# A feed-forward layer of 1728 features on a 128 x 128 array: the last 64 features as two token halves in column groups and row groups instead of one padded tile

## The chip, the cores and the metric

The kernel runs on one core of one Trainium2 chip. The metric is the device time of one execution in microseconds (us).

Names used below: PE is TensorE, PEld its weight loads, DVE is VectorE, ACT is ScalarE, POOL is GpSimd. The stationary operand of a matmul is the one that a weight load brings in; the other is the moving one. Results land in one of eight PSUM banks (`ps[:, b, :]`), which this program takes again only after DVE or ACT has emptied it. "L608" is line 608 of the kernel file; a line can be that of a helper that records all matmul groups, so the operand names matter more than the line.

## The reference, cut to what matters

```python
# S = 2048 tokens, D = 640, F = 1728 = 13 * 128 + 64
def _A_ref(x, wqkv, wo):            # linear attention with 32 heads of 20 features
    ...
    return o.reshape(B, S, D) @ wo
def _B_ref(x, w1, w2, w3, w4):
    h = _gelu(_layernorm(x) @ w1)
    ...                             # token shifts, @ w2, residual: x1
    h2 = _gelu(_layernorm(x1) @ w3) @ w4      # 640 -> 1728 -> 640
    return x1 + h2
out = g * a + (1 - g) * b           # g: a gate for each token
```

The change concerns the line with `w3` and `w4`. The hidden size 1728 is 13 full tiles of 128 features and one tile of 64.

## The kernel before

All instructions are recorded in Python, ordered by a list scheduler at build time, and then issued in that fixed order. Matmuls go through one helper. The scheduler's items name what they must follow: `(item, 0.3)` means "0.3 us after that item by the scheduler's own estimate", `(item, None)` means "after it in program order, without a delay".

```python
    def mm_group(out_ap, pairs, reads_extra=()):
            ...
            for i, (l, r) in enumerate(pairs):
                ins = e.matmul(out_ap, l, r, start=(i == 0), stop=(i == n - 1))   # L608
```

The hidden layer is padded to FP = 1792 (KF = 14 tiles, zeros in the last 64 columns of w3 and rows of w4). One w3 group is 5 matmuls of 512 tokens (KD = 5). One w4 tile of 128 tokens is 14 matmuls of 512 output columns and 14 of 128.

```python
    def w3_group(c, j):                       # c: chunk of 512 tokens, j: F tile
        cols = slice(512 * c, 512 * (c + 1))
        ...
        b = bank()
        mm_group(ps[:, b, :], [(w3[:, k, 128 * j:128 * (j + 1)], xnT[:, k, cols]) for k in range(KD)])
        activation(h2T[:, sl, j, :], ps[:, b, :], ACTF.Gelu_apprx_tanh)

    def w4_tile(t):                           # t: tile of 128 tokens
        ...
        b1, b2 = bank(), bank()
        mm_group(ps[:, b1, 0:512], [(h2T[:, sl, k, 128 * a:128 * (a + 1)], w4[:, k, 0:512]) for k in range(KF)])
        mm_group(ps[:, b2, 0:128], [(h2T[:, sl, k, 128 * a:128 * (a + 1)], w4[:, k, 512:D]) for k in range(KF)])
        stt(x_tok[:, t, 0:512], ps[:, b1, 0:512], ...)      # DVE empties the banks
        stt(x_tok[:, t, 512:D], ps[:, b2, 0:128], ...)
```

Next to w4 runs the end of the attention branch. For each token tile DVE normalizes the attention features (`qn_tile`), a DMA transposes them into `pqnT`, and PE multiplies them by `M_sb` (`a_tile`). From tile 4 on, `qn_tile(t)` may start only after `w4_tile(t - 4)`:

```python
    def qn_tile(t):
        tt(dve, qprod[:, :], pq_tok[:, t, :], zb[:, :], ALU.mult)
        ...                                   # reduce, add, reciprocal, multiply: all DVE
        sch.dma("sp", pqnT[:, :, 128 * t:128 * (t + 1)], pq_tok[:, t, :], ..., transpose=True)

    for t in range(NT):
        deps = [(("zb",), 1.0), (("q", max(t, 2)), 2.0), (("w2", NT - 1), 0.5)]
        deps.append((("w3", 0, 3 * t), 0.0) if t < 4 else (("w4", t - 4), 0.0))
        IT.add("QN", ("qn", t), 0.0, lambda t=t: qn_tile(t), deps)
```

## Time and profile before

The kernel before took 269.9 us as the median of 3 runs (269.23 to 270.06).

TensorE is busy 98% of the 268.0 us span and is 94% of the chain. Everything else has slack.

The costliest PE groups of the page: line, engine, operation, operands, shapes, count | busy us, mean ns of one | idle time just before them and what ended most of it.

```profile
L608 PE MATMUL ps<-xnT,w_60 128*128 128x512 bf16 x280 | 63.0, 379 | 0.0
L608 PE MATMUL ps<-w_85,h2T 128*128 128x512 bf16 (+1 forms) x448 | 63.0, 299 | 0.0
L608 PE MATMUL ps<-M_sb,pqnT 128*128 128x512 bf16 (+1 forms) x160 | 24.0, 299 | 0.9 <-DMA pqnT<-pq_tok 0.9
```

The first is w3 (4 chunks x 14 tiles x 5), the second w4 (16 tiles x 28), the third the attention tail. The mean of 379 ns is not what a matmul costs. Matmuls overlap, and what counts is the distance from start to start. The time-ordered view of PE shows it (start us, length us, engine, line, operands, count, and in brackets idle time before):

```profile
133.79 2.75 PE L608 MATMUL ps<-xnT,w_60 128*128 128x512 bf16 x12
...
167.25 0.87 PE L608 MATMUL ps<-M_sb,pqnT 128*128 128x512 bf16 x7
169.04 0.82 PE L608 MATMUL ps<-M_sb,pqnT 128*128 128x512 bf16 x3 [0.93 <-DMA pqnT<-pq_tok]
```

Twelve matmuls in 2.75 us are eleven distances and one duration: (2.75 - 0.38) / 11 = 0.215 us each for 512 columns. In the records a matmul of 128 columns has a distance of 56 ns. Both agree with the formula for an isolated warm matmul, N/2.4 + 2.5 ns, which the Trainium skill gives in "TensorE: Matmul & The Clock Gate", section "Back-to-back issue gap".

The waits of PE in the whole run (what it waited for: us in total, times, longest):

```profile
PE ps L828 <- POOL ones_c L662: 1.6, 1, 1.6
PE ps L608 <- DMA pqnT<-pq_tok: 0.9, 1, 0.9
PE ps L851 <- DMA wq<-in_A_wqkv_dram: 0.2, 1, 0.2
```

The first and last belong to the start. In the 250 us after it, PE waits once, for the transposed tile 4 of `pqnT`. The chain of waits shows the way to it (start us, length us, what):

```profile
163.35 0.74 DVE qprod L636
...
165.57 0.82 DVE pq_tok L1021
166.40 0.03 DVE x_tok L642
166.42 2.58 DMA pqnT<-pq_tok
169.00 0.05 issue
169.04 95.37 PE ps L608 x610
```

Tile 4 of `qn` must follow w4 tile 0, and the scheduler has placed it behind the emptying of w4 tile 1 in DVE's order (the step just before `qprod` in this chain, `x_tok` at 163.00, not shown). After `qprod` come four more DVE instructions and a DMA of 2.58 us. The matmuls at 169.04 need the result.

### The profile page before, as it was taken

Reading aid. Unit: us, or ns where it says so; the run is one execution under the profiler, and the core shown is the slowest. Engines: PE = TensorE matmul, PEld = TensorE weight load, DVE = VectorE, ACT = ScalarE, POOL = GpSimd, SP = SyncE. Lnnn points to the kernel's source line nnn. Section 1 sums busy time; section 2 is a strip of 40 time slices with the busy share of each in tenths; the row PEclk is TensorE's granted clock in tenths of the full one; section 3 lists DMA queues with packets and bytes.
Section 4 is the critical chain, followed back from the end, with each engine's and each line's share of the span. In section 5 each row is a group of like instructions: output and inputs, shape, how many; then the busy total and the mean of one; then the engine's idle time right before and its main releaser. Section 6 shows DMA issues by size and latency. Waiting matters only on the chain.

```text
span 268.0 us, 4324 instructions
## 1 busy us (share of the span) xinstructions
PE 262.3 (98%) x1707; PEld 138.9 (52%) x1707; DVE 155.0 (58%) x308; ACT 95.9 (36%) x184; POOL 102.4 (38%) x155
## 2 busy tenths in 40 slices
PE   7999999999999999999999999899999999999995
PEld 3555555555454556554444455455455455555563
DVE  1497877830005667994009957988663574374733
ACT  1396677743453451614555300003311322230000
POOL 5003995766579294965950020310111011012110
PEclk9999999999999999999999999999999999999999
DMA  6765896649568121414468210214201210310421
GB/s 185 255 100 146 193 182 121 191 82 120 103 122 285 72 49 27 96 26 53 91 141 270 51 24 0 51 24 131 42 1 24 81 55 15 27 24 0 102 72 49
DMA packets 50212, 24.69 MB, mean 92 GB/s; under 512 B 41676, under 2 KB 48781, under 8 KB 50192
## 3 DMA queue, kind: packets, MB, share of 16 engines
q1 hardware_dynamic: 49040, 21.15, 34.8%
q0 software_dynamic: 1152, 3.28, 5.3%
q8 instruction: 13, 0.21, 0.4%
q14 instruction: 7, 0.06, 0.1%
HBM read 11.96 MB, written 2.62 MB: 54 GB/s over the span
## 4 chain that ended last, share of the span: by engine, by line
PE 94%; DMA 3%; DVE 2%; SPq 1%; issue 0%
PE ps L608 84%; PE ps L779 8%; DMA wq<-in_A_wqkv_dram 2%; DMA pqnT<-pq_tok 1%; PE ps L851 1%; SPq L284 1%; PE ps L929 1%; DVE x_tok L642 1%; DVE dnr L1016 0%; DVE pq_tok L1021 0%; DVE qprod L636 0%; PE ps L619 0%; DVE dnr L1020 0%; DVE dnr L630 0%
## 5 line engine op out<-in xcount | busy, mean ns | idle before, releaser
L659 ACT ACTIVATE h2T<-ps 128x512 bf16<-128x512 f32 x56 | 33.4, 597 | 88.3 <-PE ps L608 88.3
L608 PE MATMUL ps<-xnT,w_60 128*128 128x512 bf16 x280 | 63.0, 379 | 0.0
L608 PE MATMUL ps<-w_85,h2T 128*128 128x512 bf16 (+1 forms) x448 | 63.0, 299 | 0.0
L630 POOL TENSOR_SCALAR abx<-x_tok,stg 128x640 f32<-128x640 bf16 x16 | 15.3, 959 | 108.8 <-DVE x_tok L642 37.2
L608 PEld LDWEIGHTS ps<-w_85,h2T 128*128 128x128 bf16 x448 | 35.2, 98 | 28.1
L608 PEld LDWEIGHTS ps<-xnT,w_60 128*128 128x128 bf16 x280 | 26.7, 98 | 29.4
L642 DVE SCALAR_TENSOR_TENSOR x_tok<-ps,stg,abx 128x512 bf16<-128x512 f32 (+1 forms) x32 | 17.2, 549 | 34.5 <-PE ps L608 34.2
L636 DVE TENSOR_TENSOR x_tok<-ps,x_tok 128x512 bf16<-128x512 f32 (+1 forms) x32 | 15.5, 485 | 33.8 <-PE ps L608 32.0
L659 ACT ACTIVATE Er<-ps 128x640 bf16<-128x640 f32 x32 | 22.4, 704 | 19.2 <-PE ps L608 9.8
L659 ACT ACTIVATE hsT<-ps 128x512 bf16<-128x512 f32 (+1 forms) x32 | 18.9, 594 | 24.9 <-PE ps L608 24.5
L608 PE MATMUL ps<-M_sb,pqnT 128*128 128x512 bf16 (+1 forms) x160 | 24.0, 299 | 0.9 <-DMA pqnT<-pq_tok 0.9
L779 PE MATMUL ps<-pk_tok,x_tok 128*128 128x512 bf16 (+1 forms) x160 | 24.2, 299 | 0.0
L608 PE MATMUL ps<-wkg,xT 128*128 128x512 bf16 (+1 forms) x160 | 24.0, 299 | 0.0
L608 PE MATMUL ps<-xnT,w_61 128*128 128x512 bf16 x100 | 23.9, 379 | 0.0
L608 PE MATMUL ps<-w_62,hsT 128*128 128x512 bf16 (+1 forms) x160 | 23.9, 299 | 0.0
L608 PE MATMUL ps<-wq,xT 128*128 128x128 bf16 (+1 forms) x140 | 21.1, 299 | 0.0
L642 DVE SCALAR_TENSOR_TENSOR abx<-ps,stg,abx 128x512 f32<-128x512 f32 (+1 forms) x32 | 17.6, 549 | 6.2 <-PE ps L608 2.4
L636 POOL TENSOR_TENSOR zacc<-zacc,pk_tok 128x640 f32<-128x640 f32 x15 | 20.9, 1396 | 0.4
L608 PEld LDWEIGHTS ps<-M_sb,pqnT 128*128 128x128 bf16 x160 | 13.2, 98 | 12.4 <-DMA pqnT<-pq_tok 1.1
L608 PEld LDWEIGHTS ps<-w_62,hsT 128*128 128x128 bf16 x160 | 13.3, 98 | 12.1
L608 PEld LDWEIGHTS ps<-wkg,xT 128*128 128x128 bf16 x160 | 12.9, 97 | 9.4
L779 PEld LDWEIGHTS ps<-pk_tok,x_tok 128*128 128x128 bf16 x160 | 12.6, 98 | 8.8
(67 smaller groups left out, 248.2 us busy)
## 6 DMA issues: line engine op xcount, KB each, us to landing
w_60<-in_B_w_dram SPq DMA_DIRECT2D x1, 2160.0 KB, 8.1
w_85<-in_B_w_dram SPq DMA_DIRECT2D x1, 2080.0 KB, 8.8
x_tok<-in_A_x_dram SPq DMA_DIRECT2D x3, 640.0 KB, 6.3
out_dram<-x_tok SPq DMA_DIRECT2D x3, 640.0 KB, 3.4
wq<-in_A_wqkv_dram SPq DMA_DIRECT2D x5, 160.0 KB, 4.8
wkg<-in_A_wqkv_dram SPq DMA_DIRECT2D x1, 800.0 KB, 7.3
wv<-in_A_wqkv_dram POOLq DMA_DIRECT2D x1, 800.0 KB, 6.5
wo_aug<-in_A_wo_dram POOLq DMA_DIRECT2D x5, 150.0 KB, 5.0
```

Source lines behind the costliest of these rows:

```text
L284: return e.dma_start(out_ap, in_ap)
L608: ins = e.matmul(out_ap, l, r, start=(i == 0), stop=(i == n - 1))
L630: return engf(lambda e: e.tensor_scalar(out_ap, in_ap, s1, s2, op0, op1), rd, [out_ap], cost=cost)
L636: return engf(lambda e: e.tensor_tensor(out_ap, a, b_, op), [a, b_], [out_ap], cost=cost)
L642: return dve(lambda e: e.scalar_tensor_tensor(out_ap, in0, scalar, in1, op0, op1), rd, [out_ap], cost=cost)
L659: return act(lambda e: e.activation(out_ap, in_ap, func, bias=bias, scale=scale), rd, wr, cost=cost)
L779: ins = e.matmul(o, l, r, start=(t0 + q_ == 0), stop=(t0 + q_ == NT - 1))
L851: ins = e.matmul(o, l, r, start=(k == 0), stop=(k == KD - 1))
L929: ins = e.matmul(o, l, r_, start=st_, stop=sp_, skip_group_check=True)
```

## The change

The intent is to stop multiplying by zeros. The last 64 features fill half of the array, so the other half can work on other tokens at the same time:

- **w3**: the 64 columns of w3 are the stationary operand, once in columns 0 to 63 and once in columns 64 to 127 of the array. Two matmuls of 256 tokens each run side by side. Their results land in two partition halves of one bank.
- **w4**: the contraction has 64 rows. The first token half uses rows 0 to 63, the second rows 64 to 127, with the last 64 rows of w4 loaded twice. One block serves two token tiles and starts four PSUM banks; those banks are held until the 13 full tiles have been added.
- A small third part holds the pair of banks of the kv product until they have been masked.

The diff, cut to its core:

```diff
-KF = FP // 128          # 14
+KFF = F // 128          # 13
+    h2h = rb.alloc("h2h", [128, 2, 256], BF16)
-    w4 = rb.alloc("w4", [128, KF, D], BF16)
+    w4 = rb.alloc("w4", [128, KFF + 1, D], BF16)
...
     def kvt_group(h):
         b = pair()
+        bank_hold.update((b, b + 1))        # released in lt_evac
...
+    def w3_half(c):
+        b = bank()
+        for k in range(KD):
+            xv = xnT[:, k, 512 * c:512 * (c + 1)].rearrange("p (n h q) -> p n h q", h=2, q=128)
+            for par in range(2):
+                jobs.append((ps[64 * par:64 * par + 64, b, 0:256], w3[:, k, 128 * KFF:F], xv[:, :, par, :], ...))
+        ...
+                ins = e.matmul(o, l, r, start=st, stop=sp)                          # L1026
+        activation(h2h[:, sl, :], ps[:, b, 0:256], ACTF.Gelu_apprx_tanh)
...
+    def w4_half(t):                          # t even: tiles t and t + 1
+        bs = [bank() for _ in range(4)]      # all four held
+        for i, (n0, n1) in enumerate(((0, 512), (512, D))):
+            for par in range(2):
+                rows = slice(64 * par, 64 * par + 64)
+                jobs.append((ps[:, bs[2 * par + i], 0:n1 - n0], h2h[rows, sl, 128 * pr:128 * (pr + 1)], w4[rows, KFF, n0:n1]))
+        ...
+                ins = e.matmul(o, l, r, start=True, stop=False)                     # L1078
...
     def w4_tile(t):
-        b1, b2 = bank(), bank()
+        b1, b2 = w4_banks.pop(t)             # 13 tiles, start=False                # L1096
...
-        dma_in(w4[0:64, KF - 1, :], B_w4[128 * (KF - 1):F, :], "w4b")
+        dma_in(w4[0:64, KFF, :], B_w4[128 * KFF:F, :], "w4b")
+        dma_in(w4[64:128, KFF, :], B_w4[128 * KFF:F, :], "w4c")
...
+        IT.add("W3", ("w3h", c), 0.76, lambda c=c: w3_half(c))
+        if t % 2 == 0:
+            IT.add("W4", ("w4h", t), 0.49, lambda t=t: w4_half(t), deps=deps4)
```

The operand `w3_half` reads for a token half is every second block of 128 tokens (index `h` in the rearrangement), so that each w4 half block finds two neighbouring token tiles in the two partition halves of `h2h`.

More of the change, by code (lines that the diff above doesn't have):

```diff
@@ L13 @@
 F = 1728
-FP = 1792
 H = 32
@@ L485, in _build @@
     lr = pa.alloc("lr", [128, NT, 2], F32)
-    w3 = pa.alloc("w3", [128, KD, FP], BF16)
+    w3 = pa.alloc("w3", [128, KD, F], BF16)
     w1 = pa.alloc("w1", [128, KD, D], BF16)
@@ L509, in _build @@
     pk_tok = ra.alloc("pk_tok", [128, NT, D], BF16)
-    h2T = rb.alloc("h2T", [128, 2, KF, 512], BF16)
-    w4 = rb.alloc("w4", [128, KF, D], BF16)
+    h2T = rb.alloc("h2T", [128, 2, KFF, 512], BF16)
+    h2h = rb.alloc("h2h", [128, 2, 256], BF16)
+    w4 = rb.alloc("w4", [128, KFF + 1, D], BF16)
     abx = rb.alloc("abx", [128, 4, D], F32)
@@ L727, in _build @@
     memset(pool, hsT[:, :, S:S + 4], 0.0)
-    memset(pool, w3[:, :, F:FP], 0.0)
     tags = {}
@@ L942, in lt_evac @@
             tt(dve, Lt[0:n, pi, a0 - 128 * j:a1 - 128 * j], src, msk, ALU.mult)
+        bank_hold.difference_update((b, b + 1))
     def nrow(r):
@@ L1010, in w3_group, with fn @@
         activation(h2T[:, sl, j, :], ps[:, b, :], ACTF.Gelu_apprx_tanh)
+    def w3_half(c):
+        sl = c % 2
+        b = bank()
+        jobs = []
+        for k in range(KD):
+            xv = xnT[:, k, 512 * c:512 * (c + 1)].rearrange("p (n h q) -> p n h q", h=2, q=128)
+            for par in range(2):
+                jobs.append((ps[64 * par:64 * par + 64, b, 0:256], w3[:, k, 128 * KFF:F], xv[:, :, par, :],
+                             k == 0, k == KD - 1))
+        def fn(e):
+            ins = None
+            for o, l, r, st, sp in jobs:
+                ins = e.matmul(o, l, r, start=st, stop=sp)
+            return ins
+        pe(fn, [w3[:, :, 128 * KFF:F], xnT[:, :, 512 * c:512 * (c + 1)]], [ps[:, b, 0:256]], cost=KD * 112.0 + 200.0)
+        activation(h2h[:, sl, :], ps[:, b, 0:256], ACTF.Gelu_apprx_tanh)
     def qn_tile(t):
@@ L1037, in a_tile, with fn @@
         stt(abx[:, sa, 512:D], ps[:, b2, 0:128], stg[:, 2, t:t + 1], abx[:, sa, 512:D], ALU.mult, ALU.add)
+    w4_banks = {}
+    def w4_half(t):
+        sl = (t // 4) % 2
+        tag_chk("h2T", sl, t // 4)
+        pr = (t % 4) // 2
+        bs = [bank() for _ in range(4)]
+        for i in range(4):
+            bank_hold.add(bs[i])
+        w4_banks[t] = (bs[0], bs[1])
+        w4_banks[t + 1] = (bs[2], bs[3])
+        jobs = []
+        for i, (n0, n1) in enumerate(((0, 512), (512, D))):
+            for par in range(2):
+                rows = slice(64 * par, 64 * par + 64)
+                jobs.append((ps[:, bs[2 * par + i], 0:n1 - n0], h2h[rows, sl, 128 * pr:128 * (pr + 1)], w4[rows, KFF, n0:n1]))
+        def fn(e):
+            ins = None
+            for o, l, r in jobs:
+                ins = e.matmul(o, l, r, start=True, stop=False)
+            return ins
+        pe(fn, [h2h[:, sl, 128 * pr:128 * (pr + 1)], w4[:, KFF, :]], [j[0] for j in jobs], cost=490.0)
     def w4_tile(t):
@@ L1044, in w4_tile, with grp, fn @@
         a = t % 4
-        b1, b2 = bank(), bank()
-        mm_group(ps[:, b1, 0:512], [(h2T[:, sl, k, 128 * a:128 * (a + 1)], w4[:, k, 0:512]) for k in range(KF)])
-        mm_group(ps[:, b2, 0:128], [(h2T[:, sl, k, 128 * a:128 * (a + 1)], w4[:, k, 512:D]) for k in range(KF)])
+        b1, b2 = w4_banks.pop(t)
+        def grp(o, n0, n1):
+            prs = [(h2T[:, sl, k, 128 * a:128 * (a + 1)], w4[:, k, n0:n1]) for k in range(KFF)]
+            def fn(e):
+                ins = None
+                for i, (l, r) in enumerate(prs):
+                    ins = e.matmul(o, l, r, start=False, stop=(i == KFF - 1))
+                return ins
+            pe(fn, [x_ for p_ in prs for x_ in p_], [o], cost=KFF * ((n1 - n0) * 0.4167 + 2.5))
+        grp(ps[:, b1, 0:512], 0, 512)
+        grp(ps[:, b2, 0:128], 512, D)
+        bank_hold.discard(b1)
+        bank_hold.discard(b2)
         stt(x_tok[:, t, 0:512], ps[:, b1, 0:512], stg[:, 3, t:t + 1], abx[:, sa, 0:512], ALU.mult, ALU.add)
@@ L1057, in w4_load @@
     def w4_load():
-        memset(pool, w4[:, KF - 1, :], 0.0)
-        dma_in(w4[:, 0:KF - 1, :], B_w4[0:128 * (KF - 1), :].rearrange("(k p) f -> p k f", p=128), "w4a")
-        dma_in(w4[0:64, KF - 1, :], B_w4[128 * (KF - 1):F, :], "w4b")
+        dma_in(w4[:, 0:KFF, :], B_w4[0:128 * KFF, :].rearrange("(k p) f -> p k f", p=128), "w4a")
+        dma_in(w4[0:64, KFF, :], B_w4[128 * KFF:F, :], "w4b")
+        dma_in(w4[64:128, KFF, :], B_w4[128 * KFF:F, :], "w4c")
     GEL = 1.3
@@ L1088, in _build @@
     for c in range(NCH):
-        for j in range(KF):
+        for j in range(KFF):
             deps = []
@@ L1110, in _build @@
         IT.add("AT", ("a", t), 1.33, lambda t=t: a_tile(t), deps)
-        deps4 = [(("a", t), 0.0), (("w3", c, KF - 1), GEL)]
-        IT.add("W4", ("w4", t), 3.73, lambda t=t: w4_tile(t), deps=deps4)
+        deps4 = [(("a", t), 0.0), (("w3h", c), GEL)]
+        if t % 2 == 0:
+            IT.add("W4", ("w4h", t), 0.49, lambda t=t: w4_half(t), deps=deps4)
+        IT.add("W4", ("w4", t), 3.5, lambda t=t: w4_tile(t), deps=deps4)
         if t in OUT_AT:
```

## The prediction

> **What bounds the kernel now.** TensorE. The page's busy table gives PE 98% of a 268.0 us span, and the chain of waits is 94% PE. In the time-ordered record, matmuls start every 216 ns (512 moving columns) or 56 ns (128), almost without a break from 10 us on. The waits view has one PE wait after that: 0.9 us at 168 us, for the transposed pqnT tile. The granted clock is full. So the change is worth what it does to the sum of matmul start-to-start times, to that wait, and to waits for PSUM banks.
>
> **What it removes.** The 14th F tile: 64 real features padded to 128.
> - w3: 4 chunks x 5 matmuls x 216 ns = 1.08 us a chunk, 4.3 us in all.
> - w4: 16 token tiles x (216 + 56) ns = 4.35 us.
>
> **What it adds.**
> - w3: per chunk 10 matmuls of 64 output columns x 256 tokens, in two column groups. If the two of a pair run at once, a pair costs about half of 216 ns plus a few, say 111 ns: 0.56 us. If not, 1.08 us.
> - w4: per two tiles 4 matmuls of 64 rows in two row groups: 216 + 56 + about 8 = 0.28 us if pairs overlap; if not, 0.54 us.
> - Mode switches. The Trainium skill, "TensorEngine Tiling (Array Packing)", section Key Properties, says a change of tiling mode drains the array. This trace agrees: from 128 to 40 columns the start-to-start time is 146 instead of 53 ns, coming back 112 instead of 25; from 120 to 40 rows 312 instead of 216, back 319 instead of 216. So 0.1 us each way, 0.2 us a block, 12 blocks: 2.4 us, over half of the gross gain.
>
> **Net.** w3: 1.08 - (0.56 + 0.20) = 0.32 us x 4 = 1.3 us. w4: 0.544 - (0.28 + 0.20) = 0.06 us x 8 = 0.5 us. All on the critical path. The wait at 168 us runs from the end of w4 tile 1 over DVE (qn of tile 4) and a DMA to a-tile 4; that chain keeps its 6.0 us, while PE gets one w4 half block (0.48) more and 0.27 us less under it, so the wait shrinks by 0.2 us. Sum: 2.0 us of 269.9, 0.7%.
>
> **Neutral.** Two memsets fewer on POOL, shorter gelu of the half tile (ACT has 36% load), 80 KB more w4 load, holding the kv banks (order of a few blocks near 102 us). Four PSUM banks are held for each pair of w4 tiles; DVE and ACT empty the other four behind 1.08 to 3.5 us of PE work, so I expect no new bank wait over 0.3 us.
>
> **Predicted** 268.0 us, 8 in 10 between 267.1 and 269.7. Faster by over 2%: 1%; within 2%: 96%; slower by over 2%: 3%.
>
> **What would show it.** Right: pairs of 64-column and of 64-row matmuls start a few ns apart, a w3 half block takes 0.72 to 0.80 us, a w4 half block 0.45 to 0.52, PE stays 98% busy, the wait for pqnT is about 0.7 us. Wrong: pairs start 109 or 216 ns apart (then w3 half 1.29, w4 half 0.74 us, and the kernel is some 2.4 us slower, near 272).
>
> **What would make it wrong.** No overlap of pairs; weight loads of 64 columns that do not hide under a 107 ns matmul (a pair then 130 to 160 ns, w3's gain gone); switches dearer than 0.1 us; PE waiting for one of the four banks that a w4 half block needs at once, most likely where DVE is in the 3 us of a qn tile.

## More of the kernel before

The page of the profiled run of the kernel before, in excerpt. The first line is busy time, share of the span and instruction count for each engine. The second is the granted PE clock in 40 slices (9 is 90% or more). The third is the traffic of the queue that fetches instructions (packets, MB, share of the 16 DMA engines). The fourth is the chain of work that ended last, by engine.

```profile
PE 262.3 (98%) x1707; PEld 138.9 (52%) x1707; DVE 155.0 (58%) x308; ACT 95.9 (36%) x184; POOL 102.4 (38%) x155
PEclk9999999999999999999999999999999999999999
q8 instruction: 13, 0.21, 0.4%
PE 94%; DMA 3%; DVE 2%; SPq 1%; issue 0%
```

## The result, and the profile after

The changed kernel took 268.64 us as the median of 4 runs (268.47 to 269.05), the kernel before in the same rounds 269.81 us (4 runs, 269.23 to 270.06). The ratio is 0.9962 with a 95% interval of 0.9942 to 0.9982: the same within 2%, and a little faster. A ratio here is taken from the means of the runs of both kernels in the same rounds, so it is not quite the ratio of the medians. Executions over 1.5% slower than the fastest of the same kernel are left out of the means. Five more rounds later (run e0_after) gave 268.94 us against 269.62 us, ratio 0.9978 (0.9964 to 0.9992).

The page of the kernel after, the lines that answer to those of before (busy time; chain by engine):

```profile
PE 259.9 (97%) x1727; PEld 136.4 (51%) x1727; DVE 154.2 (58%) x308; ACT 95.1 (36%) x184; POOL 101.2 (38%) x153
PE 93%; DMA 3%; DVE 2%; SPq 1%; issue 0%
```

PE lost 2.4 us of busy time while the span lost only 1.0 us: it waits more, 0.7 us of it for `pqnT` and 0.9 us at the start, for its first inputs (1.1 us there in all, instead of 0.2 us). The PE groups of the kernel after:

```profile
L1096 PE MATMUL ps<-w_86,h2T 128*128 128x512 bf16 (+1 forms) x416 | 58.9, 299 | 0.0
L608 PE MATMUL ps<-xnT,w_60 128*128 128x512 bf16 x260 | 58.7, 379 | 0.0
L608 PE MATMUL ps<-M_sb,pqnT 128*128 128x512 bf16 (+1 forms) x160 | 23.9, 299 | 1.6 <-DMA pqnT<-pq_tok 1.6
L1078 PE MATMUL ps<-w_86,h2h 64*128 64x512 bf16 (+1 forms) x32 | 3.6, 301 | 0.0
L1026 PE MATMUL ps<-xnT,w_60 128*64 128x256 bf16 x40 | 2.9, 278 | 0.0
```

w3 and w4 have 20 and 32 full matmuls fewer, and 40 and 32 small ones stand in their place (128*64 is an array of 128 rows and 64 columns, 64*128 one of 64 rows). The idle time before the attention tail is 1.6 us where it was 0.9 us. The time-ordered view of PE shows one w3 half block, one w4 half block, and that wait:

```profile
134.69 0.74 PE L1026 MATMUL ps<-xnT,w_60 128*64 128x256 bf16 x10
135.36 1.25 PE L608 MATMUL ps<-xnT,w_60 128*128 128x512 bf16 x5
...
154.61 0.45 PE L1078 MATMUL ps<-w_86,h2h 64*128 64x512 bf16 x4
154.99 1.04 PE L1096 MATMUL ps<-w_86,h2T 128*128 128x512 bf16 x4
...
166.73 0.87 PE L608 MATMUL ps<-M_sb,pqnT 128*128 128x512 bf16 x7
169.25 0.82 PE L608 MATMUL ps<-M_sb,pqnT 128*128 128x512 bf16 x3 [1.65 <-DMA pqnT<-pq_tok]
```

The next matmul starts 0.67 us after the first of the ten matmuls of 256 tokens. The single records behind these lines give the anatomy of the two blocks:

- **w3 half block.** The two matmuls of a pair start 3 to 4 ns apart. From pair to pair it is 109 ns (130 for the first). The matmul of 512 columns ahead of the block is followed after 309 instead of 216 ns, and the last pair of the block after 205 instead of 109. With both changes of mode counted in, the block costs 0.762 us in place of 1.08.
- **w4 half block.** The pairs again start 3 to 4 ns apart, the entry costs 95 ns (311 instead of 216) and the exit 92. Sum 0.473 us in place of 0.544.

So a change between the full array and a half array cost 0.092 to 0.096 us in either direction. The Trainium skill says in "TensorEngine Tiling (Array Packing)", section "Key Properties", that changing the tiling mode drains the TensorE; this trace agrees in that each change costs time, and adds the size. (Whether the array really runs empty can't be seen here: the next matmul starts 309 ns after one whose recorded length is 379 ns, and the ends in the records are modelled.) It says in "TensorE: Matmul & The Clock Gate", Part 3, that matmuls of different tiles start about 4 ns apart; this trace agrees as well, with 3 to 4 ns, for column pairs and for row pairs.

Summed over all matmul records from the first matmul with `pk_tok` (at 20.8 us) to the last one, the two traces compare so (us; my sums of start-to-start distances):

| part | before | after | difference |
|---|---|---|---|
| streaming at N/2.4 + 2.5 ns | 242.36 | 238.23 | -4.13 |
| changes of mode: 6 old ones, 24 new ones | 0.6 | 0.6 + 2.27 | +2.3 |
| distance too long at the `pqnT` wait | 1.09 | 1.81 | +0.72 |
| everything else | 0.1 | 0.3 | +0.2 |
| sum | 244.15 | 243.22 | -0.93 |

The array saved what it should. 0.7 us went into a longer wait for `pqnT`. The chain of waits of the kernel after shows that neither DVE nor the start of the DMA was late:

```profile
162.62 0.74 DVE qprod L636
...
164.84 0.82 DVE pq_tok L1040
165.66 0.03 DVE qprod L636
165.69 3.51 DMA pqnT<-pq_tok
169.20 0.05 issue
```

The DMA was issued 0.73 us earlier than before (165.69 against 166.42), and landed 0.20 us later, as it took 3.51 instead of 2.58 us. The DMA traffic between 165.6 and 169.3 us shows what else was under way. First the kernel before, then the kernel after (queue, kind: packets, MB, share of the 16 engines):

```profile
q1 hardware_dynamic: 672, 0.16, 22.6%
```

```profile
q1 hardware_dynamic: 672, 0.16, 51.2%
q8 instruction: 1, 0.02, 1.9%
```

The same 672 packets took more than twice the engine time, and one packet of 16 KB of the instruction queue lies in the same window. In the packet records of the kernel after it starts at 166.545 us and takes 1.126 us. 18 of the transposing packets of 256 B take 0.79 to 1.07 us each, where the median is 18 ns; they start around the end of the fetch (167.39 to 167.68 us) and all end within 40 ns of each other, at 168.46 to 168.49 us. The kernel before has no such packet in its transfer. (The records don't name the DMA engine of a packet, so that the slow packets stood on the fetch's engine is not shown.) The kernel before has its fetch of that place in the program at 170.11 us, after the DMA had landed.

Why did it move? The profile counts 13 such fetches in both kernels, and on average 252 to 256 TensorE instructions (matmuls and weight loads) lie between two of them, 210 to 298 in single cases. The Trainium skill says in "Runtime: NRT & Kernel Launch", section "Instruction fetch mechanics", that each engine's sequencer refills its instruction buffer in 16 KiB blocks of 256 instructions through its own DMA queue; this trace agrees for queue 8 (13 packets of 16,384 bytes), but the 7 packets of the other instruction queue, 14, have 8,192 bytes each during the run. Ahead of this fetch the change puts 24 more TensorE instructions: twice 10 for the two w3 half blocks (10 matmuls with 10 weight loads in place of 5 with 5), and 4 for the w4 half block. So the same fetch comes due earlier: in both traces it starts when TensorE has begun 2,177 of its matmuls and weight loads, but the waiting matmul of tile 4 has 2,167 ahead of it before and 2,191 after.

### The profile page after: what moved, and what is told of

The parts are those of the page before. It is cut to its first block, busy times and chain, and to the rows that moved or that the text cites. A ratio compares the mean times of both kernels' runs of the same rounds, so it can differ in the third digit from the quotient of the medians.

```text
span 267.0 us, 4369 instructions
## 1 busy us (share of the span) xinstructions
PE 259.9 (97%) x1727; PEld 136.4 (51%) x1727; DVE 154.2 (58%) x308; ACT 95.1 (36%) x184; POOL 101.2 (38%) x153
## 3 DMA queue, kind: packets, MB, share of 16 engines
HBM read 12.04 MB, written 2.62 MB: 55 GB/s over the span
## 4 chain that ended last, share of the span: by engine, by line
PE 93%; DMA 3%; DVE 2%; SPq 1%; issue 0%
PE ps L608 62%; PE ps L1096 20%; PE ps L778 8%; DMA wq<-in_A_wqkv_dram 2%; DMA pqnT<-pq_tok 1%; PE ps L1078 1%; PE ps L1026 1%; PE ps L850 1%; SPq L283 1%; PE ps L929 1%; DVE x_tok L642 1%; DVE dnr L1035 0%; DVE pq_tok L1040 0%; DVE qprod L636 0%; PE ps L619 0%
## 5 line engine op out<-in xcount | busy, mean ns | idle before, releaser
L659 ACT ACTIVATE h2T<-ps 128x512 bf16<-128x512 f32 x52 | 31.1, 597 | 84.4 <-PE ps L608 84.4
L1096 PE MATMUL ps<-w_86,h2T 128*128 128x512 bf16 (+1 forms) x416 | 58.9, 299 | 0.0
L608 PE MATMUL ps<-xnT,w_60 128*128 128x512 bf16 x260 | 58.7, 379 | 0.0
L1096 PEld LDWEIGHTS ps<-w_86,h2T 128*128 128x128 bf16 x416 | 32.5, 98 | 27.6 <-issue 1.8
L608 PEld LDWEIGHTS ps<-xnT,w_60 128*128 128x128 bf16 x260 | 24.7, 98 | 27.5 <-DVE abx L642 0.3
L608 PE MATMUL ps<-xnT,w_61 128*128 128x512 bf16 x100 | 23.9, 379 | 0.0
```

The source lines that it names most:

```text
L659: return act(lambda e: e.activation(out_ap, in_ap, func, bias=bias, scale=scale), rd, wr, cost=cost)
L1096: ins = e.matmul(o, l, r, start=False, stop=(i == KFF - 1))
```

## The experiments

The theory to test ("theory A"): the array part of the prediction is right, and the instruction fetch that falls on the transposing DMA makes the `pqnT` wait longer. The rival: the new order itself makes that wait longer (DVE, POOL or another transpose standing closer to it), or the switches, the four held banks or the weight loads of 64 columns took the missing microsecond. The kernels ran with runs of the kernel before on the same chip, 9 to 11 of them: e0 to e3 (before: 269.62 us as the median), e3b, e4, e5 and e9 (269.83 us), e6, e7 and e11 (269.71 us), and e8 (269.76 us).

All twelve runs gave correct results. "Trace span" below is the time from the first matmul with `pk_tok` to the start of the last matmul of the profiled execution: 244.15 us before, 243.22 us after. It leaves out the start, which differs between runs by some tenths. What is left repeats closely: less the time at the `pqnT` wait, the first run after, e0 and e1 have 241.41 us each. So differences of 0.1 us between trace spans can be read, though each is from one execution.

### e0_after: the changed kernel, once more

No edit.

> The changed kernel once more, on the chip of the next three runs, so that they can be compared with it. Every theory: ratio to the kernel before 0.996; the wait of TensorE for the transposed pqnT tile near 167 us about 1.8 us start to start beyond the normal 56 ns, its DMA 3.5 us from issue to landing.

Measured: 268.94 us (268.57 to 269.61, 5 runs), ratio 0.9978 (0.9964 to 0.9992). In its profiled run the fetch starts at 166.579 us, again inside the DMA, which took 3.23 us (3.5 expected), and PE waits 1.4 us for `pqnT` (1.53 us beyond the normal distance, 1.8 expected). The trace span is 242.94 us. The collision came back in a second profiled run, a little smaller.

### e1_after_shift: the same kernel, the fetches moved

Twenty tiny matmuls (16 columns) are added to the two warm-ups at the start of the kernel, where PE waits for data anyway. They change nothing near 166 us, but each fetch behind them comes due 40 TensorE instructions earlier.

```diff
-    def warmup(n, cyc):
+    def warmup(n, cyc, tiny=0):
...
+            for _ in range(tiny):
+                ins = e.matmul(ps[:, b, 0:16], ones_c[:, 0:128], ones_c[:, 128:144], start=True, stop=True)
-        addA(("warm",), 0.0, lambda: warmup(NWARM, 427.0))
+        addA(("warm",), 0.0, lambda: warmup(NWARM, 427.0, 10))
-        addA(("warm2",), 0.0, lambda: warmup(NWARM2, 300.0))
+        addA(("warm2",), 0.0, lambda: warmup(NWARM2, 300.0, 10))
```

> The changed kernel with 20 tiny matmuls (40 TensorE instructions) added to the warm-up, where TensorE waits for loads anyway. Theory A (a 16 KB fetch of TensorE instructions sits on one DMA engine ahead of that transposing DMA): the fetch comes 40 instructions earlier, near 164 us, before the DMA is issued at 165.7; the DMA takes 2.6 us again, the wait falls from 1.8 to about 0.9 us, the kernel is about 0.9 us faster than the changed kernel (ratio to before 0.9925 to 0.994). Theory B (the wait grew because VectorE's order or the number of queued transposes changed): nothing of that moves, wait 1.8 us, ratio 0.996.

Measured: 267.74 us (267.45 to 268.18, 6 runs), ratio 0.9933 (0.992 to 0.9946), so 20 added matmuls made the kernel 1.2 us faster than e0_after. The fetch now starts at 162.95 us, before the DMA. The chain of waits has the DMA at its old length, and the view of PE's waits has the wait of the size that was predicted:

```profile
165.51 2.57 DMA pqnT<-pq_tok
```

```profile
PE ps L608 <- DMA pqnT<-pq_tok: 0.7, 1, 0.7
```

What follows: the collision with the fetch is the cause of the longer DMA and of the longer wait. The new order with the fetch elsewhere has a wait of 0.7 us. The distance at this wait explains 0.7 us of the gain over e0 and 0.9 us of the gain over the first run after, and that is the whole difference of the trace spans (242.28 us against 242.94 and 243.22). The rest of the 1.2 us of the medians lies outside the trace span: in the profiled runs the first matmul with `pk_tok` starts 0.3 us earlier in e1 (20.58 against 20.88 us). Why was not found; over all traces it starts at 20.58 to 21.20 us.

### e2_before_shift: the kernel before, its fetch moved onto the DMA

The same edit on the kernel before with 6 + 6 tiny matmuls, so that its fetch falls into the DMA.

```diff
-        addA(("warm",), 0.0, lambda: warmup(NWARM, 427.0))
+        addA(("warm",), 0.0, lambda: warmup(NWARM, 427.0, 6))
-        addA(("warm2",), 0.0, lambda: warmup(NWARM2, 300.0))
+        addA(("warm2",), 0.0, lambda: warmup(NWARM2, 300.0, 6))
```

> The kernel before with 12 tiny matmuls (24 TensorE instructions, about what the change adds ahead of this place) in the warm-up. Theory A: the fetch that fell at 170.1 us, after the DMA, now falls near 167 us, into it; the DMA takes about 3.5 us, the wait grows from 1.1 to about 2.0 us, the kernel is 0.7 to 1.0 us slower than before (ratio 1.0025 to 1.004). Theory B: wait 1.1 us, ratio 1.000.

Measured: 270.44 us (269.71 to 271.41, 6 runs), ratio 1.0033 (1.0015 to 1.0051), the kernel before made 0.8 us slower. The fetch starts at 168.07 us. The chain of waits, and the DMA traffic from 167.4 to 170.8 us:

```profile
167.46 3.24 DMA pqnT<-pq_tok
```

```profile
q1 hardware_dynamic: 672, 0.16, 47.4%
q8 instruction: 1, 0.02, 2.0%
```

The wait is 1.6 us instead of 0.9. What follows: the effect does not need the change. The unchanged kernel has it too, as soon as the fetch falls there. The profiled run of e2 also waited 1.0 us at 43.6 us for a transposed input (`xT`), which the others do not. Without that wait (1.13 us beyond the normal distance) its trace span is 0.67 us longer than that of before, as much as the distance at the `pqnT` wait grew (1.75 us instead of 1.09).

The other transposes of `pqnT` say the same. The 14 traces have 224 of them. The 171 that no fetch of queue 8 overlaps took 2.54 to 2.98 us. The 29 in which a fetch started 0.3 to 2.24 us after the DMA was issued took 2.83 to 4.42 us, and each of the 31 over 3 us has a fetch in it. Overlap alone is not enough: 18 of the other 24, whose fetch started earlier or later, kept 2.55 to 2.62 us.

### e3_after_qn4: tile 4 of `qn` moved ahead, to take away the wait itself

If DVE does `qn` of tile 4 before it empties w4 tile 1, the DMA is issued earlier, and a longer DMA does not matter.

```diff
-        deps.append((("w3", 0, 3 * t), 0.0) if t < 4 else (("w4", t - 4), 0.0))
+        deps.append((("w3", 0, 3 * t), 0.0) if t < 4 else (("w4", 0), None) if t == 4 else (("w4", t - 4), 0.0))
```

> The changed kernel with VectorE's work for tile 4 (qn) put ahead of the emptying of w4 tile 1, so that its DMA is issued some 3 us earlier. Both theories: TensorE no longer waits for pqnT (under 0.1 us), 1.8 us faster than the changed kernel, ratio to before about 0.989 to 0.990. If the time falls by less, a new wait (bank or VectorE) took it up.

Measured: 268.52 us (267.51 to 268.89, 6 runs), ratio 0.9955 (0.9939 to 0.997). This is a miss: the expected ratio was 0.989 to 0.990. The wait for `pqnT` is gone, and the view of PE's waits has a new one:

```profile
PE ps L1078 <- DVE abx L642: 1.3, 1, 1.3
```

It is the w4 half block of tiles 4 and 5, held up from 174.2 to 175.5 us. The scheduler had put the attention tail of tile 5 directly ahead of it. The half block wants four free banks at once, and the last of them was still being emptied by DVE. So the risk that the prediction named last is real (the Trainium skill warns of it in "TensorEngine Tiling (Array Packing)", "Gotcha 1: PSUM Pressure": row tiles write to different banks). It just didn't occur in the changed kernel, where the largest such wait was about 0.05 us.

### e3b_after_qn4: the same, and tile 5 kept away from the half block

```diff
-        deps.append((("w3", 0, 3 * t), 0.0) if t < 4 else (("w4", t - 4), 0.0))
+        deps.append((("w3", 0, 3 * t), 0.0) if t < 4 else (("w4", t - 4), None if t < 6 else 0.0))
...
+        if t == 5:
+            deps.append((("w4", 4), None))        # a-tile 5 after w4 tile 4
```

> As the run with tile 4's qn moved up, but with qn of tiles 4 and 5 right after w4 tiles 0 and 1, and the a-tile of tile 5 held back, so that no two a-tiles stand right before a w4 half block. My theory: that run lost its gain to the four banks that the w4 half block asks for at once; here neither wait is left (each under 0.15 us), ratio to before 0.989 to 0.991, 1.8 us below the changed kernel. Rival (TensorE was not the limit, the gain goes to whatever comes next): ratio stays at 0.995.

Measured: 267.19 us (266.96 to 268.64, 6 runs), ratio 0.9908 (0.9888 to 0.9929). After the start PE waits for nothing, as the whole view of its waits shows; the trace span is 241.35 us.

```profile
PE ps L827 <- POOL ones_c L662: 1.6, 1, 1.6
PE ps L850 <- DMA wq<-in_A_wqkv_dram: 0.4, 1, 0.4
```

The fetch at 167.00 us finds no wait to lengthen: the DMA of tile 4 was issued at 163.20 us and had landed.

### e4_before_qn4: the kernel before with the same move

The first of the two edits of e3b, on the kernel before (it holds no banks, so the second is not needed).

```diff
-        deps.append((("w3", 0, 3 * t), 0.0) if t < 4 else (("w4", t - 4), 0.0))
+        deps.append((("w3", 0, 3 * t), 0.0) if t < 4 else (("w4", t - 4), None if t < 6 else 0.0))
```

> The kernel before with the same moves of qn. No fetch and no half block is involved: the wait of 1.1 us goes, ratio to before 0.995 to 0.997. Against it, the run above shows what the change is worth without that wait: my sum from the start-to-start times says 4.1 us less streaming minus 2.3 us for 24 switches, 1.7 to 1.9 us, a ratio of about 0.9935 between the two.

Measured: 268.74 us (268.39 to 268.98, 6 runs), ratio 0.9958 (0.9944 to 0.9972), trace span 243.05 us, no wait after the start, although a fetch at 168.31 us met the DMA of tile 5, which took 3.95 us: it had slack. e3b and e4 are the change with the wait taken out of both sides: 1.55 us by the medians, 1.70 us by the trace spans. The prediction's sum for the array alone was 1.3 + 0.5 = 1.8 us.

### e5_unpaired: both halves on the same half of the array

On e3b: the number of matmuls and of changes of mode stays, but both halves use the same 64 columns (w3) and the same 64 rows (w4), so nothing can run side by side. (The gelu that follows works on 64 partitions then; that and the flags of the matmuls are cut.)

```diff
-                jobs.append((ps[64 * par:64 * par + 64, b, 0:256], w3[:, k, 128 * KFF:F], xv[:, :, par, :], ...))
+                jobs.append((ps[0:64, b, 256 * par:256 * par + 256], w3[:, k, 128 * KFF:F], xv[:, :, par, :], ...))
...
-                jobs.append((ps[:, bs[2 * par + i], 0:n1 - n0], h2h[rows, sl, 128 * pr:128 * (pr + 1)], w4[rows, KFF, n0:n1]))
+                q0 = 256 * par + 128 * pr
+                jobs.append((ps[:, bs[2 * par + i], 0:n1 - n0], h2h[0:64, sl, q0:q0 + 128], w4[0:64, KFF, n0:n1]))
```

> As the first of these, still without padding and with the same mode switches, but both halves of w3 go to the same 64 columns and both of w4 to the same 64 rows, one after the other. If the gain comes from running two halves at once: second matmuls start 109 ns (w3), 216 and 56 ns (w4) after the first instead of 3, a w3 half block takes some 1.28 us instead of 0.76, a w4 half block some 0.74 instead of 0.47, in all 4.2 us slower than the first, and 2.3 us slower than the kernel before with qn moved (ratio to before about 1.005). If leaving out the padding were itself the gain: no slower than the first.

Measured: 271.47 us (270.85 to 274.13, 6 runs), ratio 1.0076 (1.0041 to 1.0111), where about 1.005 was expected; one run of 274.13 us pulls the mean up; by the medians it is 1.6 us above the kernel before, a ratio of 1.006. The trace span is 245.67 us, 4.32 us more than e3b. The time-ordered view of PE has a w3 and a w4 half block without pairs:

```profile
134.89 1.28 PE L1026 MATMUL ps<-xnT,w 128*64 128x256 bf16 x10
136.10 1.25 PE L608 MATMUL ps<-xnT,w 128*128 128x512 bf16 x5
...
155.90 0.71 PE L1078 MATMUL ps<-w,h2h 64*128 64x512 bf16 x4
156.55 0.82 PE L1096 MATMUL ps<-w,h2T 128*128 128x512 bf16 x3
```

The next matmul comes 1.21 us after the first of the w3 half (0.67 us with pairs), and 0.65 us after the first of the w4 half (0.38 us with pairs): 4 x 0.54 + 8 x 0.27 = 4.3 us, as the trace spans say. What follows: the concurrency of the pairs is worth 4.3 us, and without it the change loses to the padded tile, as the switches are paid all the same.

### e6_more_switches: sixteen more changes of mode, nothing else

On e3b: the 128-column pair of the w4 half block is moved behind the 512-column group of the first tile, so each of the eight blocks enters and leaves the half array twice.

```diff
-        pe(fn, [...], [j[0] for j in jobs], cost=490.0)
+        pe(lambda e: fn(e, jobs[0:2]), ...)
+        w4_late[t] = lambda: pe(lambda e: fn(e, jobs[2:4]), ...)
...
         grp(ps[:, b1, 0:512], 0, 512)
+        if t in w4_late:
+            w4_late.pop(t)()
```

> As the changed kernel with qn of tiles 4 and 5 moved (0.9908 of before), but the 128-column pair of each w4 half block comes after the 512-column group of the first tile: the same matmuls, 16 more changes of tiling mode. If a change costs TensorE 0.09 to 0.1 us and nothing hides it: 1.4 to 1.6 us slower than that kernel, ratio to before 0.9960 to 0.9970, and 40 places with some 0.095 us beyond the streaming time where there were 24. If changes are free when the queue is full: no slower.

Measured: 268.68 us (268.44 to 268.7, 5 runs), ratio 0.996 (0.9946 to 0.9975). The trace span is 243.05 us, 1.70 us more than e3b, or 0.106 us for each added change of mode. (1.4 to 1.6 us had been expected. By the ratios it is 1.4 us, by the medians, each against its own runs of the kernel before, 1.6 us.) One of the pairs that were moved, in the time-ordered view of PE:

```profile
157.97 0.23 PE L1079 MATMUL ps<-w,h2h 64*128 64x128 bf16 x2
158.13 0.90 PE L1098 MATMUL ps<-w,h2T 128*128 128x128 bf16 x13
```

In the records each of the 16 entries costs 95 to 96 ns and each of the 16 exits 102 to 103 ns, where the eight exits of e3b's w4 half blocks cost 92 to 93. So the old exits grew a little too, and an added change by itself is about 0.1 us. This is the switch cost measured by itself; with the 24 switches of the change it is 2.3 to 2.5 us, over half of the 4.13 us of streaming that it saves.

### e7_w3_only and e8_w4_only: one part of the change alone

On e3b. In e7 the w3 part stays, and w4's last 64 rows run in the full array, with one copy of them for each token half that is padded with zeros in the other half. In e8 the w4 part stays, and the w3 group runs in the full array with the 64 columns twice, for all 512 tokens.

```diff
 e7:
-    w4 = rb.alloc("w4", [128, KFF + 1, D], BF16)
+    w4 = rb.alloc("w4", [128, KFF + 2, D], BF16)
-                jobs.append((..., h2h[rows, sl, 128 * pr:128 * (pr + 1)], w4[rows, KFF, n0:n1]))
+                jobs.append((..., h2h[:, sl, 128 * pr:128 * (pr + 1)], w4[:, KFF + par, n0:n1]))
+        memset(pool, w4[:, KFF:KFF + 2, :], 0.0)
 e8:
-        (the ten matmuls in column groups)
+        mm_group(ps[:, b, :], [(w3[:, k, 128 * KFF:F + 64], xnT[:, k, cols]) for k in range(KD)])
+        dma_in(w3[:, :, F:F + 64], B_w3[:, F - 64:F].rearrange("(k p) f -> p k f", p=128), "w3b")
```

> The same base, with the new w3 half block alone: w4's last 64 rows are again multiplied in the full array, padded with zeros (two copies, one for each half), so w4 has no row groups and no mode change. My split of the gain (w3 0.318 us x 4 = 1.27 us, w4 0.071 us x 8 = 0.57 us) says: 0.5 to 0.6 us slower than the base, 1.2 to 1.3 us faster than the kernel before with qn moved (0.9958), so ratio to before 0.9910 to 0.9930; each w4 half block 0.544 us instead of 0.473. If the four banks held for w4 cost something, or if w4 gives more than I think, the distance to the base differs.

> The counterpart of the run with the w3 half block alone: w3's last tile again in the full array (its 64 columns loaded twice, so that both row halves hold it), w4 by row groups as in the change. By my split w4 alone gives 0.071 us x 8 = 0.57 us against the kernel before with qn moved (0.9958): ratio to before 0.9930 to 0.9945, and each w3 half block 1.08 us. If the two halves of the change did not simply add up, it would lie elsewhere; near 0.9958 would say that the w4 part gives nothing.

Measured: e7 267.41 us (267.25 to 267.65, 5 runs), ratio 0.9919 (0.9906 to 0.9932), trace span 241.90 us. e8 268.08 us (267.84 to 268.45, 5 runs), ratio 0.9938 (0.9925 to 0.9952), trace span 242.57 us. The w4 half of e7 in the time-ordered view of PE takes 0.54 us from start to start, as the padded tile does:

```profile
154.59 0.70 PE L1077 MATMUL ps<-w,h2h 128*128 128x512 bf16 x4
155.13 1.24 PE L1095 MATMUL ps<-w,h2T 128*128 128x512 bf16 x5
```

(These spans come from different chips, so that the ratios to the kernel before, 0.9919 and 0.9938 against e4's 0.9958, are the check: 1.05 and 0.54 us.) Against e4 (243.05 us), the w3 part alone saves 1.15 us in the trace span, the w4 part alone 0.48 us, both together (e3b) 1.70 us. So the parts add up, w3 is worth over twice as much as w4, and the predicted sizes (1.3 and 0.5 us) hold.

### e9_merged: the four w3 half blocks as one

On e3b: the four blocks need only the transposed input, so they can stand behind each other and pay for two switches instead of eight.

```diff
-    h2h = rb.alloc("h2h", [128, 2, 256], BF16)
+    h2h = rb.alloc("h2h", [128, NCH, 256], BF16)
...
+    def w3_halves():
+        for c in range(NCH):
+            w3_half(c)
+    IT.add("W3H", ("w3h",), 2.4, w3_halves, deps=[(("t2", u), 0.9) for u in range(4 * NCH - 4, 4 * NCH)] + [(("w3", 0, KFF - 1), 0.0)])
-        IT.add("W3", ("w3h", c), 0.76, lambda c=c: w3_half(c))
...
-        deps4 = [(("a", t), 0.0), (("w3h", c), GEL)]
+        deps4 = [(("a", t), 0.0), (("w3", c, KFF - 1), GEL), (("w3h",), GEL)]
```

> As the first of these, with the four w3 half blocks done together once the last token chunk is ready: 2 switches into and out of column tiling instead of 8. If a switch costs 0.095 us wherever it stands: 0.55 to 0.65 us faster than the first (ratio to before about 0.987 to 0.989). If switches overlap with other waits: no difference.

Measured: 267.85 us (267.64 to 268.26, 6 runs), ratio 0.9929 (0.9915 to 0.9944), where 0.987 to 0.989 was expected: a miss, and slower than e3b. The new item changed the priorities of the scheduler. The wo product, which e3b has in two parts (at 111 and 118 us), now stands in one piece at 118 us, and the matmuls behind it, which don't read its result, wait for ACT, which empties it from PSUM into `M_sb`. There are more gaps, all of 0.2 to 0.6 us, between 110 and 122 us. One of them in the view of PE's waits:

```profile
PE ps L608 <- ACT M_sb L659: 0.5, 1, 0.5
```

The merged block itself came out as planned: in the records it has one entry (93 ns) and one exit (95 ns). So the time of this run says nothing against the cost of switches; it tells only that an item moved in such a scheduler can move others.

### e11_best: merged blocks with the order kept, and the wo product without a mode of its own

On e3b: the merged block is an ordinary member of the w3 stream behind chunk 1, and the dependency of w4 on it is given a lag of -1000, so that it counts for the order but not for the priorities. In addition the last 40 rows of the wo product are padded to 120 with zeros, which takes away four old changes of mode. Together that is ten changes of mode fewer.

```diff
+        if c == 1:
+            IT.add("W3", ("w3h",), 2.4, w3_halves)
-        IT.add("W3", ("w3h", c), 0.76, lambda c=c: w3_half(c))
...
-        deps4 = [(("a", t), 0.0), (("w3h", c), GEL)]
+        deps4 = [(("a", t), 0.0), (("w3", c, KFF - 1), GEL)]
+        if t == 0:
+            deps4.append((("w3h",), -1000.0))
...
+    memset(pool, wo_aug[:, 5, :], 0.0)
-        mm_group(ps[:, b1, 0:512], [(Lt[0:nrow(r), pi, :], wo_aug[0:nrow(r), r, 0:512]) for pi, r in prs])
+        mm_group(ps[:, b1, 0:512], [(Lt[0:R6, pi, :], wo_aug[0:R6, r, 0:512]) for pi, r in prs])
```

> A try for a faster version on the same base: the four w3 half blocks together in one (6 switches fewer), and in the earlier product with wo the last 40 rows padded with zeros to 120 so that the array stays in full mode (4 switches fewer), with the order elsewhere kept nearly the same. At 0.095 to 0.105 us a switch, and 0.021 us for the slower first pair of three blocks: 0.6 + 0.4 = 1.0 us faster than the base, ratio to before 0.986 to 0.988, about 266.1 us. If it is less, the changed order brought a new wait, as in the first try of the merged blocks.

Measured: 265.96 us (265.38 to 266.19, 4 runs), ratio 0.986 (0.9844 to 0.9877), the fastest of all. The merged block in the time-ordered view of PE:

```profile
150.37 2.38 PE L1026 MATMUL ps<-xnT,w 128*64 128x256 bf16 x40
```

The trace span is 240.25 us, 1.11 us less than e3b. About 0.06 us of it are the slow first pairs of three blocks, which leaves 0.105 us for each of the ten changes of mode. The traces (e6, e7, e11) lack 32 matmul records each, so sums over records are not taken from them.

## Why the prediction was right, and where it was off

The prediction was 268.0 us within 267.1 to 269.7; 268.64 and 268.94 us were measured. The range was wider than the gain, so landing in it says little; of the 1.9 us that the prediction expected, 1.2 and 0.7 us came. The points are what counts:

- **What bounds the kernel: right.** PE was 94% of the chain before and 93% after, and in the experiments that changed PE's sum of distances (e3b against e4, e5, e6, e7, e8, e11) the time moved by about as much.
- **Pairs run side by side: right.** They start 3 to 4 ns apart, and taking the concurrency away (e5) cost 4.3 us. The rival with weight loads of 64 columns that don't hide fell: they take 109 ns on the average (those of 128 columns 98 ns), and the pairs still follow each other in 109 ns.
- **Switches of 0.1 us: right.** 0.092 to 0.096 us in the changed kernel, 0.095 to 0.103 us in the records of e6, about 0.105 us in e11. The old changes of mode in the trace of before (94 ns for 120 to 40 columns and so on) were a sound measure for new ones.
- **w3 saves 0.32 us a block, w4 0.06 us: right.** 0.318 and 0.071 us in the records. By experiment 1.15 us for w3 (1.3 predicted) and 0.48 us for w4 (0.5 predicted).
- **The wait for `pqnT`: wrong, in direction and size.** The prediction said that "that chain keeps its 6.0 us" and that "the wait shrinks by 0.2 us", to about 0.7 us. It grew to 1.6 us (1.4 us in e0_after). The chain up to the DMA did keep its length, but the DMA took 3.51 instead of 2.58 us, as an instruction fetch of 16 KB fell into it. So the step that failed is "that chain keeps its 6.0 us": it took the DMA's time as fixed. That term of the sum was off by 0.9 us (0.7 us in e0_after), which is about what lies between the 268.0 us of the prediction and the 268.64 and 268.94 us measured. e1, in which only the fetches are moved, has the wait of 0.7 us and 267.74 us.
- **"PE stays 98% busy": 97%.** About half of it is the same wait; the other half is 0.9 us more of waiting for the first inputs, at the start, which no experiment looked into.
- **No new bank wait over 0.3 us: right for this order of instructions** (about 0.05 us at 247.7 us), but e3 shows how close it was: one item moved, and 1.3 us were lost for the four banks.
- **The neutral parts stayed neutral.** No wait on POOL, ACT or the w4 load shows up after the start. Holding the kv banks was not tested by itself; it's left open whether it is worth anything.

Open: where the part of e1's gain came from that the wait does not explain (about 0.5 us by the medians against e0, outside the trace span); whether the fetch collides in each execution, as only profiled executions show where it falls (it did in both profiled runs of the changed kernel, and the times of e0 and e1 don't overlap); and how a DMA engine shares its time between a 16 KB packet and packets of 256 B, as only the times of the packets are seen, and not their engines.

## What to carry to other kernels

Half tiles in row or column groups run side by side, but each block pays two changes of mode of about 0.1 us: count the blocks first, merge blocks of one mode, and compare with zero padding, which here cost only 0.27 us a pair of matmuls (512 and 128 columns) and no switch. When a kernel is bound by one engine without gaps, the gain of a change can be summed from start-to-start distances to a tenth of a microsecond, but the one wait that remains is where the result may go wrong; look there for everything that can lengthen it, also the fetch of instructions, whose place moved here with each TensorE instruction that was added ahead of it. What helped here without depending on where the fetch falls was to give the awaited transfer slack, as e3b and e4 do, and to check afterwards in the waits that no new one took its place.

## What the Trainium skill lacked or had wrong

- "TensorEngine Tiling (Array Packing)", "Key Properties", says that a change of mode drains the TensorE, but gives no size. Measured: 0.092 to 0.096 us in each direction between the full array and column or row halves, up to 0.103 us in e6. A pair of 512-column half matmuls saves 0.21 us over running them one after the other, so a lone pair hardly pays for its two switches.
- "TensorE: Matmul & The Clock Gate", Part 3, gives the span of one pack but not of a stream of packs. Measured: 109 ns from pair to pair of 256 columns, and 130 ns (21 more) for the first pair of each column block.
- The same page, "Back-to-back issue gap", gives about 131 ns for 512 columns and about 81 ns for 128 columns as the sustained spacing in a stream with weight loads, and calls N/2.4 + 2.5 ns the figure of an isolated matmul. In this kernel's streams, with a weight load (98 ns) for each matmul, the spacing was 215 to 216 ns and 55 to 56 ns: the formula held, and the sustained figures did not.
- "Runtime: NRT & Kernel Launch", "Instruction fetch mechanics", calls the cost of a block boundary mostly hidden. It was hidden from TensorE's own instruction stream (outside its waits and changes of mode, the 13 fetches of the kernel before left 0.1 us of excess distance in all), but not from others: one fetch of 16 KB took 0.9 to 1.8 us in these runs, and the transposing DMA of tile 4, 672 packets, took 3.23 to 3.51 us where it met one (the kernel after, e0, e2) instead of 2.57 to 2.58 us (before, e1), which cost PE 0.7 to 0.9 us. No page that I read names this as a cause of a late DMA.
